# Batch 1's landmark sums from the loaded k and q, paired weight conversions and a new instruction order in a Nystrom attention and two-MLP kernel

## The chip, the cores and the metric

The kernel runs on one core of a Trainium2 chip, as one launch. The metric is the device time of a run in microseconds (us). A separate profiled execution gives the trace; its span runs from the first to the last instruction on the core.

## The reference, cut to what matters

```python
def _attn_ref(q, k, v):                      # (4, 8, 576, 64) each, float32
    m, scale = 32, 1.0 / np.sqrt(D)
    q_lm = q.reshape(B, H, m, S // m, D).mean(axis=3)      # landmarks: means of 18 tokens
    k_lm = k.reshape(B, H, m, S // m, D).mean(axis=3)
    A, Bm, C = sm(q, k_lm), sm(q_lm, k_lm), sm(q_lm, k)    # softmaxes of scaled products
    Z = Bm.transpose(0, 1, 3, 2) / (norm1(Bm) * norminf(Bm) + 1e-06)
    for _ in range(6):
        Z = 2 * Z - Z @ Bm @ Z
    return A @ Z @ C @ v

x = attention output as (2304, 512)
x = ((x @ w_a) * (x @ w_b)) @ w_out          # w_a, w_b: 512x1536, w_out: 1536x512
h = x @ w_in                                 # 512x2048
out = (h * np.tanh(softplus(h))) @ w_out2    # 2048x512
```

The weights come as float64, so each is loaded as pairs of 32-bit words and turned to float32 in the kernel.

## The kernel before, in words

**Two phases.** In the first, the attention of four batches is interleaved with the first MLP. `attention(ap, b, ...)` is a set of steps for batch b: `kl` and `ql` (landmark sums of k and q), `sB`, `BB` and `NS` (the small softmax and six steps of the inverse), `sC0`, `sC1` (landmarks against all keys), `ET0`, `ET1` (transposes by the unit matrix `ident`), `U`, `M`, and `A0`, `A1`, `A0n`, `A1n` (queries against landmarks, their exponentials and the normalised result `at`). `fold` (`f0`, `f1`, `F0`, `F1`) multiplies M into a tile of w_a and w_b and gives `bm`. A slot `s0` to `s11` (`ab`) makes the products of `at` and `bm` for both weights, and `o1` multiplies their product into w_out. The second phase is the second MLP and isn't touched.

**Weights.** `u0` holds units of the first MLP's weights. A unit's words are loaded into a staging tile (`stage`) and converted by `to_f32` in five instructions: Abs on ACT, two tensor_scalar and two scalar_tensor_tensor on DVE. A w_a/w_b unit is 128x512 elements; a w_out unit (`wo1_unit`) is split into two parts as well. `c0`, `c1`, ... in the order are such units, one instruction or two at a time. The first eight staging tiles are buffers of the tag `w`, which the w_out tiles take over later; further ones use three buffers of the tag `stg`.

**Order.** `ORDER_1` is a text that writes out the instruction order on ACT, PE and DVE by hand, up to slot 11: a name runs the next piece of batch 0's step, `+name` that of batch 1's step, `cN` that of a unit; a number is that many fill products of `ident` with itself; `|` closes one PSUM pool and opens the next. Each engine takes its queue in this order, so an instruction that waits holds up those behind it on its engine. After the text a loop over slots 12 to 95 with a list of due steps goes on. All loads are issued by SP; their place in SP's queue is the framework's choice.

**Batch 1's landmark sums before.** The host hands over q and k of batch 1 a second time, in token order (`q1`, `k1`). `load_tokens` loads them as six tiles `tok`. `lm_sum` multiplies each 126x128 block of tokens as weights by a 126x7 block matrix `blk`: 40 products into one PSUM bank for k and for q, each in two instructions in the trace. For batches 0, 2 and 3 a DVE reduction of the loaded tile (`kt`, `qt`) gives the sums. `kt` has a single buffer (tag `kv`), so batch 1's k is loaded when batch 0's last sC product has read the one before. It serves sC0 and sC1.

Of the kernel before, what the change touches and what calls it, by code (L numbers as in the profile page):

```python
# [17 lines left out]
LM = 32  # L18
# [13 lines left out]
def nystrom_moe_kernel(ctx: ExitStack, tc: tile.TileContext, q, k, v, w_a, w_b, w_out1, w_in2, w_out2, q1, k1, out):  # L32
# [55 lines left out]
    blk = const.tile([128, 7], F32, name="blk")  # L88
# [17 lines left out]
    def load_qk(ap, b):  # L106
        out, step = [], 4 if b else 2
        for src, nm, tag, bufs in ((k, "kt", "kv", 1), (q, "qt", "qt", 2)):
            t = ap.tile([128, 4, S], F32, tag=tag, bufs=bufs, name=nm)
            for j in range(0, 4, step):  # L110
                nc.sync.dma_start(out=t[:, j:j + step].rearrange("p j s -> p (j s)"), in_=src[b][:, S * j:S * (j + step)])
            out.append(t)
        return out

    def load_tokens():
        out = []
        for src in (k1, q1):
            ts = []
            for i in range(0, 5, 2):
                if src is q1 and i:  # L120
                    t = main.tile([128, 2, 2, S // 2], F32R, tag="AT", bufs=6, name="tok").bitcast(F32).rearrange("p a b s -> p (a b s)")
                else:
                    t = main.tile([128, 4, 288], F32, tag="x2", bufs=4, name="tok").rearrange("p a s -> p (a s)")
                w = min(2, 5 - i)
                nc.sync.dma_start(out=t[0:126, 0:DM * w], in_=src[:, DM * i:DM * (i + w)])
                ts.append(t)
            out.append(ts)
        return out
# [20 lines left out]
    def attention(ap, b, kt, qt, vt0=None, tokens=None):  # L149
# [226 lines left out]
    N_UNITS, N_SLOTS = 20, 12  # L376
    ORDER_1 = """
        kl kl ql ql c0 sB sC0 sB c0 sB sC1 4 c1 sC0 sB c2 sC1 BB 2 sC1 c3 BB sC1 sC1 c2 NS 2 c1 c3 NS ET0 NS
        c0 NS 2 c1 ET0 ET1 c3 c1 NS A0 ET1 NS c1 NS 1 A0 U NS A0 NS A0 c3 NS +kl U NS NS A0 c3 NS c0 +kl NS A0
        c0 NS +ql c2 c2 NS A0n c4 +ql NS +ql c5 c2 A0n M c6 +kl c5 M c5 A0n c5 f0 c7 A0n A1 c7 f0 c7 +kl A1 c8  # L380
        f0 +ql +kl A1 | s0 +ql c7 A1 +sC0 c5 +sC1 +sC0 s0 s0 A1 +sC1 s1 +sC1 A1 s0 c7 c6 s1 s1 A1n s0 s0 A1n
        c6 +sC1 s1 c6 +sC1 +sB c6 A1n +ET0 +sB s1 A1n +sB s1 +ET0 +sB s2 +ET1 c4 s2 c4 +BB c4 +ET1 s2 c4 +BB
        +U s2 c8 s2 +NS +U s2 s3 +NS +NS c8 +NS c8 s3 s3 +NS +NS c9 c8 +NS s3 f1 c8 c9 +NS +NS s3 c9 +NS c8 s3
        f1 c9 +NS c10 +NS f1 +NS +NS +NS s4 c10 c9 +NS s4 c10 s4 c9 +NS s5 s4 c10 s4 +M s5 s4 c10 s5 +M c9 c10
        s6 s5 c11 c10 +A0 s6 c11 s5 s6 c11 s5 c11 c12 s7 s6 c11 F0 s7 s6 +A0 c11 s6 s7 +A0 F0 +A1 c11 +A0 s7
        o0 F0 +A0 c12 o1 c12 +A0 c12 c12 o0 c13 F1 +A0n o1 s7 o2 c13 F1 s7 +A0n F1 +A0n o3 o2 +A0n c13 s8 c13
        c14 c13 o3 o4 s8 c14 c14 c14 c15 s8 +A1 o4 s9 c15 s8 o5 s9 +A1 s8 s8 c14 +A1 s9 c15 c15 c16 s10 s9 +A1
        c16 o6 c16 c16 s10 +A1 c15 s10 c16 o5 s11 +A1n o6 c17 o7 s9 s10 s11 +A1n s9 s10 c17 +A1n s11 s10 c17
        o7 c17 +A1n c18 s11 c18 s11 c18 s11 c17 c19 c18 c19 c19 c18 c19 c19
# [65 lines left out]
    def wab_units(g):  # L455
        def conv(i, jj, st):
# [3 lines left out]
            yield from to_f32(t[:, 2 * jj:2 * jj + 2, i], st, True)  # L460
            converted[g] = converted.get(g, 0) + 1
# [14 lines left out]
    def split_unit(dst_hi, dst_lo, st):  # L476
# [22 lines left out]
    def load_wo1(c):  # L499
        wo1[c] = main.tile([128, 2, DM], F32R, tag="w", bufs=8, name="wo1")  # L500
# [202 lines left out]
    u0 = Units(sum([wab_units(2 * w) + wab_units(2 * w + 1) + [wo1_unit(4 * w + c) for c in range(4)] for w in range(3)], []), early=8)  # L703
# [321 lines left out]
```

## Time and profile before

| | |
|---|---|
| median of 3 runs | 844.27 us (842.61 to 844.44) |
| the profiled execution's own time | 844.01 us |
| its span | 842.2 us |
| PE busy | 802.5 us (95%), 5882 matmuls |
| DVE busy | 555.0 us (66%) |
| ACT busy | 360.9 us (43%) |
| DMA | 183.45 MB, mean 218 GB/s |
| mean granted TensorE clock | 0.978 |

The profiled execution takes 1.81 us more than its span: that lies around the first and last instruction. A PE that is busy isn't a PE at its peak, because matmuls overlap and their ends are modelled. "Granted clock" is a share of 2.4 GHz; 0.50 is 1.2 GHz. A line L56 is the helper that records nearly every instruction of ACT, PE and DVE, so rows are told apart by their tiles. In the rows, a `MATMUL out<-moving,weights` is written with the names of its two operands; PEld is the weight load.

### The profile page before, as it was taken

What the parts mean: (1) busy time and instruction counts of PE and PEld (TensorE: products, weight loads), DVE (VectorE), ACT (ScalarE), POOL (GpSimd) and SP (SyncE); (2) the same over time, 40 slices, a digit from 0 to 9 for tenths busy, and PEclk for the clock granted to TensorE, in tenths of its full rate; (3) what the DMA queues carried; (4) which work ended last, traced back from release to release, by engine and by line L of the source; (5) the groups of instructions that cost most, each with busy time, mean ns of one, the idle gap of its engine ahead of it and who ended that gap; (6) DMA issues with size and microseconds to landing.
All of it is one profiled execution on the core that took longest, in us unless ns stands there. A gap on an engine that the chain in (4) does not pass through costs nothing.

```text
span 842.2 us, 14866 instructions
## 1 busy us (share of the span) xinstructions
PE 802.5 (95%) x5882; PEld 701.6 (83%) x5882; DVE 555.0 (66%) x1023; ACT 360.9 (43%) x826; POOL 146.9 (17%) x141
## 2 busy tenths in 40 slices
PE   5878899999999999999998899999999999999998
PEld 4765788987887887887887798998999999999997
DVE  7678887895574488788995678768443347433433
ACT  3555865434333444444543345345332234332332
POOL 0002022222231232222234435321000000000000
PEclk9679999999999999999999899999999999999999
DMA  9957577459326438777476866789755445655502
GB/s 326 334 203 255 179 241 234 176 195 317 107 86 243 179 96 295 266 264 251 131 255 252 293 249 245 271 318 340 262 194 219 165 174 211 219 213 194 187 1 75
DMA packets 48733, 183.45 MB, mean 218 GB/s; under 512 B 4260, under 2 KB 12452, under 8 KB 39320
## 3 DMA queue, kind: packets, MB, share of 16 engines
q1 hardware_dynamic: 48664, 182.51, 61.1%
q8 instruction: 46, 0.75, 0.4%
q14 instruction: 23, 0.19, 0.1%
HBM read 129.02 MB, written 53.48 MB: 217 GB/s over the span
## 4 chain that ended last, share of the span: by engine, by line
PE 73%; DVE 12%; DMA 7%; issue 3%; ACT 3%; POOL 0%; SPq 0%; DVEq 0%; ACTq 0%
PE ps_ab L56 32%; PE ps_o L56 20%; PE ps_bm L56 11%; PE ps_at L56 10%; DVE f L56 4%; DMA wi2d<-f 2%; DMA tok<-in_q_dram 2%; ACT sa L56 1%; DMA wo2d<-f 1%; DMA stg<-in_moe_w_a_dram 1%; DVE tg L56 1%; DVE f L413 1%; DVE wab L56 1%; ACT f L409 1%; DVE s L56 1%
## 5 line engine op out<-in xcount | busy, mean ns | idle before, releaser
L56 PE MATMUL ps_ab<-xc,wc 128*128 128x384 f32 x1008 | 199.8, 338 | 4.8 <-DVE u2s L56 3.1
L56 PE MATMUL ps_ab<-at,bm 128*128 128x288 f32 x1152 | 188.6, 304 | 6.0 <-DVE tg L56 4.8
L56 PEld LDWEIGHTS ps_ab<-xc,wc 128*128 128x128 f32 x1008 | 180.4, 189 | 16.1 <-DVE u2s L56 3.4
L56 PEld LDWEIGHTS ps_ab<-at,bm 128*128 128x128 f32 x1152 | 162.2, 190 | 31.3 <-issue 8.6
L56 PE MATMUL ps_o<-g,wo 128*128 128x288 f32 x1152 | 180.4, 298 | 5.7 <-DVE x2acc L56 2.6
L56 PEld LDWEIGHTS ps_o<-g,wo 128*128 128x128 f32 x1152 | 161.0, 189 | 20.4 <-issue 8.1
L555 POOL TENSOR_TENSOR g<-tg,g 128x288 fp32r<-128x288 f32 x96 | 85.7, 893 | 330.4 <-ACT g L56 330.4
L56 ACT ACTIVATE m<-c 128x384 f32<-128x384 f32 x96 | 50.3, 524 | 183.9 <-DVE c L56 183.9
L56 PE MATMUL ps_bm<-wo,g 128*128 128x512 f32 x288 | 94.4, 392 | 0.3 <-ACT g L56 0.3
L56 PE MATMUL ps_at<-wo,g 128*128 128x512 f32 x288 | 81.8, 391 | 0.0
L56 DVE TENSOR_TENSOR g<-m,g 128x384 fp32r<-128x384 f32 x96 | 66.2, 690 | 23.5 <-ACT g L56 23.5
L56 PE MATMUL ps_o<-wo,g 128*128 128x512 f32 x288 | 78.9, 391 | 0.0
L56 ACT ACTIVATE g<-tg 128x288 fp32r<-128x288 f32 x96 | 42.4, 442 | 75.5 <-DVE tg L56 75.1
L56 DVE SCALAR_TENSOR_TENSOR f<-stg,f 128x512 uint32<-128x512 uint32 x88 | 69.9, 797 | 1.5
L56 DVE TENSOR_TENSOR tg<-ps_ab,ta 128x288 f32<-128x288 f32 x96 | 43.3, 452 | 31.2 <-PE ps_ab L56 22.8
L56 PEld LDWEIGHTS ps_at<-wo,g 128*128 128x128 f32 x288 | 54.0, 188 | 10.0
L56 PEld LDWEIGHTS ps_o<-wo,g 128*128 128x128 f32 x288 | 53.5, 188 | 8.5
L56 ACT ACTIVATE ta<-ps_ab 128x288 f32<-128x288 f32 x96 | 38.8, 404 | 49.0 <-PE ps_ab L56 48.3
L56 PEld LDWEIGHTS ps_bm<-wo,g 128*128 128x128 f32 x288 | 53.4, 189 | 6.7 <-ACT g L56 0.8
L56 ACT ACTIVATE g<-m 128x384 fp32r<-128x384 f32 x96 | 50.2, 523 | 2.6
L56 DVE TENSOR_TENSOR c<-ps_ab,m 128x384 f32<-128x384 f32 x24 | 13.4, 557 | 48.2 <-PE ps_ab L56 48.2
L409 ACT ACTIVATE f<-stg 128x512 f32<-128x512 f32 x44 | 29.7, 675 | 31.7 <-DMA wi2d<-f 12.8
(145 smaller groups left out, 815.5 us busy)
## 6 DMA issues: line engine op xcount, KB each, us to landing
wc<-wcd SPq DMA_DIRECT2D x16, 1792.0 KB, 7.2
wo<-wod SPq DMA_DIRECT2D x16, 1024.0 KB, 5.4
stg<-in_moe_w_out_dram SPq DMA_DIRECT2D x28, 512.0 KB, 3.9
wcd<-wc SPq DMA_DIRECT2D x8, 1792.0 KB, 6.1
wab<-wabd SPq DMA_DIRECT2D x10, 1024.0 KB, 5.9
stg<-in_moe_w_in_dram SPq DMA_DIRECT2D x16, 512.0 KB, 5.8
wod<-wo SPq DMA_DIRECT2D x8, 1024.0 KB
stg<-in_moe_w_a_dram SPq DMA_DIRECT2D x12, 512.0 KB, 3.8
```

The costliest lines, as they stand in the source:

```text
L56: i = f(*a, **kw)
L409: i = ac.engine.activation(dst, hi.bitcast(F32), AF.Abs)
L413: i = ve.engine.tensor_scalar(dst, dst, F32_TINY, F32_HUGE, op0=ALU.max, op1=ALU.min)
L555: gp.tensor_tensor(t[:, 1], tg, t[:, 0].bitcast(F32), op=ALU.subtract)
```

## The change

Batch 1's `kl` and `ql` no longer use a second copy of k and q. Each is 18 products, one for every token t of a block, with `ident` as the weights and the 128x128 elements `[:, j, 18 l + t]` of the loaded `kt` or `qt` as the moving operand (four rows of 32, an element every 72 bytes); they accumulate in one PSUM bank, six products to a piece of the order. `load_tokens`, `blk`, `q1` and `k1` go. Four of the units, those of w_a and w_b for groups 0 and 1, become pairs: w_a's and w_b's 128x512 words lie side by side in a staging tile of twice the size, and each of the five instructions treats 128x1024 elements. The buffers of tag `w` become four of twice the size, and w_out tiles are two halves of one buffer. `u0.n` counts units finished in order, so that units may finish out of order. `ORDER_1` is a new text, with batch 1's `kl` and `ql` later: their first piece stands just before batch 0's A1 ends, the others after s0 has begun. Before, all of them but the last pieces stood ahead of s0.

```diff
-    blk = const.tile([128, 7], F32, name="blk")
...
-        ve.tensor_reduce(out=blk, in_=ident[:, 0:126].rearrange("p (l k) -> p l k", k=BLK), axis=AX, op=ALU.add)
...
-    def load_tokens():
-        out = []
-        for src in (k1, q1):
...
         def lm_sum(src, nm):
             x[nm] = sm([128, 4, LM], nm)
-            if tokens:
-                p, ts = bank("o1"), tokens[nm == "ql"]
-                for j in range(4):
-                    for i in range(5):
-                        n, r = (4, 72) if i == 4 else (7, 126)
-                        f0 = DM * (i % 2) + 128 * j
-                        pe.matmul(p[:, LM * j + 7 * i:LM * j + 7 * i + n], ts[i // 2][0:r, f0:f0 + 128], blk[0:r, 0:n], start=True, stop=True)
-                    yield
+            if b == 1:
+                p = bank("o1")
+                for t in range(BLK):
+                    pe.matmul(
+                        p[:, 0:128].rearrange("p (j l) -> p j l", l=LM), ident, src.rearrange("p j (l k) -> p k j l", k=BLK)[:, t],
+                        start=(t == 0), stop=(t == BLK - 1),
+                    )
+                    if t % 6 == 5:
+                        yield
                 ac.activation(x[nm].rearrange("p j l -> p (j l)"), p[:, 0:128], AF.Copy)
                 return
...
-    N_UNITS, N_SLOTS = 20, 12
+    N_UNITS, N_SLOTS = 16, 12
     ORDER_1 = """
-        kl kl ql ql c0 sB sC0 sB c0 sB sC1 4 c1 sC0 sB c2 sC1 BB 2 sC1 c3 BB sC1 sC1 c2 NS 2 c1 c3 NS ET0 NS
-        c0 NS 2 c1 ET0 ET1 c3 c1 NS A0 ET1 NS c1 NS 1 A0 U NS A0 NS A0 c3 NS +kl U NS NS A0 c3 NS c0 +kl NS A0
-        c0 NS +ql c2 c2 NS A0n c4 +ql NS +ql c5 c2 A0n M c6 +kl c5 M c5 A0n c5 f0 c7 A0n A1 c7 f0 c7 +kl A1 c8
-        f0 +ql +kl A1 | s0 +ql c7 A1 +sC0 c5 +sC1 +sC0 s0 s0 A1 +sC1 s1 +sC1 A1 s0 c7 c6 s1 s1 A1n s0 s0 A1n
...
+        kl kl ql ql sB sC0 sB sB sC1 4 sC0 c0 sB sC1 BB 2 sC1 c1 BB sC1 c0 NS 2 sC1 c0 NS NS ET0 c1 ET1 c0 ET0
+        NS 2 ET1 A0 c1 NS U NS A0 A0 c2 NS 1 c1 NS A0 NS c0 NS NS A0 NS c1 NS NS A0 NS U NS NS c3 A0n M M A0n
+        f0 c2 A0n A1 c3 f0 A0n f0 +kl A1 A1 | s0 +kl c2 s0 A1 c3 s0 c2 A1 +ql s0 c2 A1 +ql c3 +kl c4 s0 A1n
+        +ql s0 +kl A1n s1 +ql c3 +sC0 A1n s1 +sC1 +sC0 s1 +sC1 +sC1 A1n +sC1 s1 s2 +sC1 c4 c4 +sB s1 c4 f1 s2
...
     def stage(src, shape, early):
 
-        tag, bufs = ("w", 8) if early else ("stg", 3)
-        t = (main if early else base).tile([128, 512, 2], U32, tag=tag, bufs=bufs, name="stg")
+        if early:
+            t = main.tile([128, 2 * DM, 2], U32, tag="w", bufs=4, name="stg2")
+            v = t.rearrange("p (j i f) w -> p j i (f w)", j=2, i=2)
+            for i, a in enumerate(src):
+                nc.sync.dma_start(out=v[:, :, i], in_=a)
+            return t
+        t = base.tile([128, 512, 2], U32, tag="stg", bufs=3, name="stg")
...
-            yield from to_f32(t[:, 2 * jj:2 * jj + 2, i], st, True)
-            converted[g] = converted.get(g, 0) + 1
+            half = t[:, 2 * jj:2 * jj + 2]
+            yield from to_f32(half.rearrange("p j i f -> p (j i f)") if double else half[:, :, i], st, True)
+            converted[g] = converted.get(g, 0) + 1 + double
...
+    def wo1_tile(c):
+        if c % 2 == 0:
+            wo1_two[0] = main.tile([128, 2, 2, DM], F32R, tag="w", bufs=4, name="wo1")
+        wo1[c] = wo1_two[0][:, c % 2]
...
-    u0.prefetch(4)
-    vt0 = load_v(ap, 0)
-    tokens = load_tokens()
-    u0.prefetch(8)
+    u0.prefetch(2)
+    vt0 = load_v(ap, 0)
+    u0.prefetch(4)
     run0 = attention(ap, 0, kt, qt, vt0)
-    run1 = attention(ap, 1, *load_qk(ap, 1), None, tokens)
-    u0.prefetch(11)
+    run1 = attention(ap, 1, *load_qk(ap, 1))
+    u0.prefetch(7)
...
     def unit(n):
         yield from u0.units[n][2](u0.st[n])
-        u0.n = n + 1
-        if n > 7:
+        finished.add(n)
+        while u0.n in finished:
+            u0.n += 1
+        if n > 3:
             u0.prefetch(3)
```

## Rows read from the trace of the kernel before

**Rows 1.** Windows: start and end us, length, busy us of each engine, clock, DMA share, GB/s.
```profile
18.00:30.00 12.00, 9.74 (x200) 7.79 (x198) 9.50 (x24) 7.65 (x44) 0.00 (x0) 0.88 1.04 243
30.00:46.00 16.00, 16.00 (x108) 13.29 (x108) 9.11 (x19) 5.42 (x10) 0.00 (x0) 0.50 1.01 403
...
45.66:119.00 73.34, 62.81 (x670) 49.50 (x671) 63.10 (x135) 49.27 (x184) 11.28 (x13) 0.94 0.58 200
...
119.00:842.00 723.00, 705.12 (x4783) 624.20 (x4781) 460.96 (x815) 292.67 (x579) 134.32 (x116) 0.99 0.60 212
```

**Rows 2.** Chain that ended last, in order of time: start us, us, what.
```profile
13.44 15.94 DMA tok<-in_q_dram
...
29.43 1.59 PE ps_o L56 x6
...
31.38 4.36 PE ps_o L56 x20
...
41.45 4.36 PE ps_o L56 x20
45.80 1.65 PE ps_ab L56 x6
```

**Rows 3.** Tile `tok`: duration of one in ns (min/median/max), first and last start.
```profile
L56 PEld LDWEIGHTS ps_o<-blk,tok x80: 186/333/337, 23.1 to 45.4; 126*128 126x128 f32 x64, 72*128 72x128 f32 x16
L56 PE MATMUL ps_o<-blk,tok x80: 252/360/382, 23.1 to 45.4; 126*128 126x7 f32 x64, 72*128 72x4 f32 x16
```

**Rows 4.** Timeline of SP, then the DMA issues of 0 to 60 us (KB, us to landing).
```profile
27.11 3.62 SPq L399 DMA_DIRECT2D stg<-in_moe_w_out_dram  x3
31.67 0.33 SPq L111 DMA_DIRECT2D kt<-in_k_dram  x1
...
kt<-in_k_dram SPq DMA_DIRECT2D x1, 1152.0 KB, 13.9
```

**Rows 5.** Timeline, batch 0's last steps ahead of slot 0: start us, us, instructions.
```profile
26.55 0.22 DVE L56 TENSOR_TENSOR rz<-ps_at,rz 128x64 f32<-128x64 f32 x1
...
28.01 0.20 ACT L56 ACTIVATION_READ_ACCUMULATOR sa<-sa,stA 128x1 f32 x1
...
30.95 0.44 PE L56 MATMUL ps_at<-rz 32*32 32x32 f32 x16
...
38.53 1.96 PE L56 MATMUL ps_bm<-wab,mt 64*32 64x512 f32 x16
...
40.59 1.02 ACT L56 ACTIVATE bm<-ps_bm 128x1024 fp32r<-128x1024 f32 x1 [2.74 <-PE ps_bm L56]
...
42.32 1.19 DVE L56 TENSOR_TENSOR bm<-ps_bm,bm 128x1024 fp32r<-128x1024 f32 x1
```

**Rows 6.** Timeline of weight loads: fill products of 128 columns, then one stretch of `tok`.
```profile
7.55 2.64 PEld L56 LDWEIGHTS ps_o<-kl,ident 128*128 128x128 f32 x12 [7.55 <-issue]
...
12.87 1.20 PEld L56 LDWEIGHTS ps_o<-ident 128*128 128x128 f32 x8 [0.92 <-PE ps_p L56]
...
31.31 4.34 PEld L56 LDWEIGHTS ps_o<-blk,tok 126*128 126x128 f32 x20
```

**Rows 7.** Timeline of DVE, two reductions of the unit matrix.
```profile
1.51 0.28 DVE L56 TENSOR_REDUCE blk<-ident 128x7 f32<-128x126 f32 x1 [1.51 <-POOL ident masks.py:199]
1.71 0.36 DVE L56 TENSOR_REDUCE ist<-ident 128x32 f32<-128x128 f32 x1
```

**Rows 8.** Timeline of PE, the first and last of five waits between 53 and 66 us.
```profile
56.24 0.30 PE L56 MATMUL ps_at<-kl,ql 64*32 64x32 f32 x16 [3.38 <-ACT E L56]
...
65.86 0.43 PE L56 MATMUL ps_at<-rz 32*32 32x64 f32 x16 [0.90 <-DVE U L56]
```

**Rows 9.** Windows, two microseconds just after the longest of those waits.
```profile
58.00:60.00 2.00, 1.70 (x8) 1.60 (x8) 1.86 (x8) 0.65 (x4) 1.00 (x1) 0.50 0.00 0
```

**Rows 10.** Groups of DVE by form: busy us, mean ns of one, idle before.
```profile
L56 DVE SCALAR_TENSOR_TENSOR wab<-stg,wab 128x512 uint32<-128x512 uint32 x11 | 7.4, 687 | 0.1
...
L56 DVE TENSOR_TENSOR bm<-ps_bm,bm 128x1024 fp32r<-128x1024 f32 x5 | 6.1, 1212 | 0.0
```

More of the change, by code (lines that the diff above doesn't have):

```diff
@@ L31, in nystrom_moe_kernel @@
 @with_exitstack
-def nystrom_moe_kernel(ctx: ExitStack, tc: tile.TileContext, q, k, v, w_a, w_b, w_out1, w_in2, w_out2, q1, k1, out):
+def nystrom_moe_kernel(ctx: ExitStack, tc: tile.TileContext, q, k, v, w_a, w_b, w_out1, w_in2, w_out2, out):
     nc = tc.nc
@@ L112, in load_qk @@
             out.append(t)
-        return out
-    def load_tokens():
-        out = []
-        for src in (k1, q1):
[L118 to L127, printed above, removed]
         return out
@@ L147, in nystrom_moe_kernel, with attention @@
     PAIRS1 = {"ET0": "bm", "ET1": "bm"}
-    def attention(ap, b, kt, qt, vt0=None, tokens=None):
+    def attention(ap, b, kt, qt, vt0=None):
         x = {}
@@ L371, in attention @@
         return run
-    N_UNITS, N_SLOTS = 20, 12
+    N_UNITS, N_SLOTS = 16, 12
     ORDER_1 = """
-        kl kl ql ql c0 sB sC0 sB c0 sB sC1 4 c1 sC0 sB c2 sC1 BB 2 sC1 c3 BB sC1 sC1 c2 NS 2 c1 c3 NS ET0 NS
-        c0 NS 2 c1 ET0 ET1 c3 c1 NS A0 ET1 NS c1 NS 1 A0 U NS A0 NS A0 c3 NS +kl U NS NS A0 c3 NS c0 +kl NS A0
-        c0 NS +ql c2 c2 NS A0n c4 +ql NS +ql c5 c2 A0n M c6 +kl c5 M c5 A0n c5 f0 c7 A0n A1 c7 f0 c7 +kl A1 c8
-        f0 +ql +kl A1 | s0 +ql c7 A1 +sC0 c5 +sC1 +sC0 s0 s0 A1 +sC1 s1 +sC1 A1 s0 c7 c6 s1 s1 A1n s0 s0 A1n
[L382 to L389, printed above, removed]
@@ new lines, in nystrom_moe_kernel @@
+        +NS c5 s4 +ET1 s3 c5 +NS +U s4 +NS c5 +NS c4 s4 c5 s4 c6 +NS +U s5 +NS +NS c6 +NS s5 c6 s5 +NS +NS c7
+        c6 +NS s5 s6 +NS +NS s5 c7 +NS c7 s5 s6 s6 +NS c8 s7 c7 s6 +M s7 c7 s7 +M s6 c6 +A0 c7 s6 s7 c6 F1 c7
+        s7 +A0 s7 F1 +A0 +A1 F1 +A0 c6 F0 +A0 c8 c8 o0 +A1 +A0 c8 F0 +A0n o1 o0 c9 F0 o2 o1 +A0n +A1 +A0n o3
+        o2 +A0n +A1 c9 s8 c9 o3 c8 o4 s8 c9 c10 c9 +A1 s8 c10 c10 o4 s9 s8 +A1 c10 o5 c10 s9 s8 +A1n s9 s8 o5
+        c11 +A1n s10 s9 o6 +A1n c11 s10 c11 s9 c11 c12 s9 s10 c11 o6 s11 c12 s10 o7 c12 s11 c12 s10 c13 s10
@@ L390, in nystrom_moe_kernel @@
+        c12 s11 o7 c13 c13 s11 c13 s11 +A1n s11 c14 c13 c14 c14 c14 c15 c14 c15 c15 c15 c15
     """
     def stage(src, shape, early):
-        tag, bufs = ("w", 8) if early else ("stg", 3)
-        t = (main if early else base).tile([128, 512, 2], U32, tag=tag, bufs=bufs, name="stg")
+        if early:
[4 more added lines that the diff above has]
+            return t
@@ L453, in nystrom_moe_kernel, with wab_units @@
     wabd = [dram.tile([128, 2048], F32, name=f"wabd{g}") for g in range(6)]
-    def wab_units(g):
+    def wab_units(g, double=False):
         def conv(i, jj, st):
@@ L466, in wab_units @@
         for jj in range(2):
-            for i, w in enumerate((w_a, w_b)):
-                src = w.bitcast(U32)[256 * jj:256 * jj + 256, 512 * g:512 * g + 512].rearrange("(j p) f -> p j f", p=128)
-                out.append((src, 2, lambda st, i=i, jj=jj: conv(i, jj, st)))
+            two = [w.bitcast(U32)[256 * jj:256 * jj + 256, 512 * g:512 * g + 512].rearrange("(j p) f -> p j f", p=128) for w in (w_a, w_b)]
+            if double:
+                out.append((two, 2, lambda st, jj=jj: conv(0, jj, st)))
+            else:
+                for i, src in enumerate(two):
+                    out.append((src, 2, lambda st, i=i, jj=jj: conv(i, jj, st)))
         return out
@@ L485, in split_unit @@
         yield
-        (gp if u0.n == 36 else ve).tensor_tensor(dst_lo, f3, dst_hi.bitcast(F32), op=ALU.subtract)
-    wo1 = {}
+        (gp if u0.n == 32 else ve).tensor_tensor(dst_lo, f3, dst_hi.bitcast(F32), op=ALU.subtract)
+    wo1, wo1_two = {}, [None]
+    def wo1_tile(c):
+        if c % 2 == 0:
+            wo1_two[0] = main.tile([128, 2, 2, DM], F32R, tag="w", bufs=4, name="wo1")
+        wo1[c] = wo1_two[0][:, c % 2]
     wo1d = [dram.tile([128, 2, DM], F32, name=f"wo1d{c}") for c in range(12)]
@@ L492, in conv @@
         def conv(st):
-            wo1[c] = main.tile([128, 2, DM], F32R, tag="w", bufs=8, name="wo1")
+            wo1_tile(c)
             yield from split_unit(wo1[c][:, 0], wo1[c][:, 1], st)
@@ L499, in load_wo1 @@
     def load_wo1(c):
-        wo1[c] = main.tile([128, 2, DM], F32R, tag="w", bufs=8, name="wo1")
+        wo1_tile(c)
         nc.sync.dma_start(out=wo1[c].bitcast(F32), in_=wo1d[c])
@@ L702, in nystrom_moe_kernel @@
     consts()
-    u0 = Units(sum([wab_units(2 * w) + wab_units(2 * w + 1) + [wo1_unit(4 * w + c) for c in range(4)] for w in range(3)], []), early=8)
+    u0 = Units(sum([wab_units(2 * w, w == 0) + wab_units(2 * w + 1, w == 0) + [wo1_unit(4 * w + c) for c in range(4)] for w in range(3)], []), early=4)
+    u0.prefetch(2)
+    vt0 = load_v(ap, 0)
     u0.prefetch(4)
-    vt0 = load_v(ap, 0)
-    tokens = load_tokens()
-    u0.prefetch(8)
     run0 = attention(ap, 0, kt, qt, vt0)
-    run1 = attention(ap, 1, *load_qk(ap, 1), None, tokens)
-    u0.prefetch(11)
+    run1 = attention(ap, 1, *load_qk(ap, 1))
+    u0.prefetch(7)
     def fill(n):
@@ L716, in fill @@
             pe.matmul(p[:, 0:128], ident, ident, start=True, stop=True)
+    finished = set()
     def unit(n):
         yield from u0.units[n][2](u0.st[n])
-        u0.n = n + 1
-        if n > 7:
+        finished.add(n)
+        while u0.n in finished:
+            u0.n += 1
+        if n > 3:
             u0.prefetch(3)
@@ L1012 @@
         args.append(nc.dram_tensor(f"in_{name}_dram", a.shape, _mybir.dt.from_np(a.dtype), kind="ExternalInput").ap())
-    for name in "qk":
-        a = _np.pad(inputs[name].reshape(B, H, S, D)[1].transpose(1, 0, 2).reshape(S, DM), ((0, 54), (0, 0)))
-        a = arrays[f"in_{name}1_dram"] = _np.ascontiguousarray(a.reshape(5, 126, DM).transpose(1, 0, 2)).reshape(126, 5 * DM)
-        args.append(nc.dram_tensor(f"in_{name}1_dram", a.shape, _mybir.dt.from_np(a.dtype), kind="ExternalInput").ap())
     for i, (shape, dtype) in enumerate(_OUTS):
```

1 line of the change is left out of this document (added).

## The prediction

> **What bounds the kernel now.** I read the windows first. From 119 us, where the written order ends, to the last instruction TensorE is busy 705.12 of 723 us at a granted clock of 0.99 [rows 1]. Nothing in that part is touched, so a microsecond won or lost before it moves the end by about a microsecond. Ahead of it the picture is worse: between 18 and 30 us the DMA engines are full but move only 243 GB/s, and between 30 and 46 us TensorE is busy all the time, at 0.50 of its clock [rows 1].
>
> The chain says what that busy time is. From 13.44 to 29.38 us the last chain runs through the load of `tok`, then through `tok` products on TensorE, 20 of their instructions at a time, until the first product of slot 0 at 45.80 us in the chain's count [rows 2]. So batch 1's landmark sums hold the start of batch 0's slots. The tile view shows the price: 80 instructions between 23.1 and 45.4 us, with a median weight load of 333 ns [rows 3]. A stretch of 20 lasts 4.34 us, 0.217 us each [rows 6], so the 80 take up to 17.4 us.
>
> **What goes.** Three things leave the way to slot 0. First, 2,520 KB of `tok` loads: 126 rows x 5 blocks x 2,048 bytes, twice, or 2.58 MB. At the 243 GB/s of the time in which they move [rows 1] that is 10.6 us of transfers. Second, up to 17.4 us of TensorE. Third, the wait that these put on batch 0. Its fifth inverse step is finished by DVE at 26.77 us, but the sixth, in the same queue behind `tok` products that wait for data, starts at 30.95 us [rows 5]: 4.2 us lost. The fold's products start at 38.53 us, and its result is ready on DVE at 43.51 us [rows 5].
>
> Without `tok`, the sixth step can run at 26.8 us. Behind it the order needs its closing DVE work, M and MT (about 2 us), while ACT's last exponential of A0, which ends at 28.21 us [rows 5], releases A0n. I put the fold's start at 29.2 us. It needs 1.96 us on TensorE at the low clock, 1.02 on ACT and 1.19 on DVE [rows 5], 4.2 in all: `bm` is ready at about 33.5 us. That is the early bound for slot 0.
>
> The late bound comes from k. The first piece of `+kl` stands ahead of A1's end and of s0 on TensorE, and it now needs batch 1's `kt`. This load was issued at 31.67 us behind three w_out loads, and landed 13.9 us later [rows 4], at 45.6 us. With the `tok` transfers gone from the full DMA stretch it lands 10.6 us earlier, at 35.0 us; if it also goes ahead of the three w_out loads (1,536 KB, 3.9 us at the 403 GB/s of rows 1's second window) at 31.1 us. Behind it stand six products, 12 instructions, at 0.22 us (below): 2.6 us. So slot 0 starts between 33.7 and 37.6 us. I take the middle, 35.6 us, and against 45.66 us that is **10.0 us earlier** (8.1 to 12.0).
>
> **What comes.** 36 products with the unit matrix, each two instructions like the fill products, 72 in all. The trace has such products of 128 columns with a contiguous operand: eight weight loads in 1.20 us, 0.15 us each, and at the start twelve in 2.64 us, 0.22 us each [rows 6]. The strided operand isn't in the trace. Below, a read could be as cheap as the contiguous one, and I see no reason for less than 0.15 us. Above, the nearest rows are two DVE reductions of nearly as many elements: 0.28 us in contiguous order, 0.36 us with a step of 32 elements [rows 7], which is 29% more (it also writes 32 outputs where the other writes 7). By twice the price an instruction takes 0.30 us. I take 0.185 us, the middle of 0.15 and 0.22, because part of these products run at the low clock and a step may cost something.
>
> Six of the 36 stand ahead of s0 and are in its start above. The other 30, 60 instructions, stand among s0 and s1 and cost 60 x 0.185 = 11.1 us (9.0 to 18.0). From 45.66 to 119 us TensorE is idle 10.5 us of 73.34 [rows 1]. These products depend on nothing but k and q, so they fill waits they stand near. The five waits between 53 and 66 us, the first of 3.38 us and the last of 0.90 [rows 8], add up to 5.7 us, and I count these as filled. That leaves **5.3 us of lengthening**. Bounds: none, if all 10.5 us take them in at 9.0; 12.3, if a product costs 0.30 us. Filling the gap of 3.38 us should also spare the fall of the clock after it: at 58 to 60 us TensorE was busy 1.70 us at 0.50 [rows 9], of which half is lost, 0.85 us. I count **0.8 us back** (0 to 1.5).
>
> **Pairs.** A DVE instruction on 128x512 takes 687 ns, one on 128x1024 takes 1,212 [rows 10], so merging two saves about 0.16 us: four DVE instructions in four pairs, 2.6 us. I cost it at nothing. Over half of it lies ahead of slot 0, where DVE is busy 9.11 of 16 us [rows 1], and TensorE, not DVE, sets the pace there. Behind slot 0 it is about 1 us, and the new order leaves DVE about as much more conversion to do there (before, three more DVE steps of c5 and two of c7 stood ahead of `|`; now two first steps of pairs do). DVE is busy 63.10 of 73.34 us in that stretch [rows 1], so this cover is thin: if DVE were the bound, a microsecond would count either way. A pair also holds DVE's queue for up to 1.2 us, with batch 0's small inverse steps behind it; before, two units in succession held it as long.
>
> **At nothing, too.** The `blk` reduction (0.28 us) ran at 1.51 us [rows 7], before any k had come. The w_out tiles in halves of one buffer: the two halves are used by one `o1` piece and fall free together; if one load waited for the other's release, slots of the loop behind cover it. Units finished out of order change only when the next staging tile is loaded; DMA is full only 0.58 of that stretch [rows 1]. `kt` is held longer, and v of batch 1 loads into its buffer later, by the few us that sC1 comes later relative to s0.
>
> **Sum.** 10.0 - 5.3 + 0.8 = 5.5 us. From the profiled execution's own time of 844.0 us, of which 842.2 are span, that gives **838.5 us**. The median of the runs shown is 0.26 us above that execution, so the same number stands for both.
>
> **Rivals.** *The strided read takes twice as long.* Every element of the operand lies 72 bytes from the next, and rows 7 show that an engine can pay for steps. At 0.30 us the 60 instructions are 18.0 us, 12.3 beyond the five waits: 10.0 - 12.3 + 0.8 leaves a loss of 1.5 us, 845.5 us. Against it: at 0.22 us and the low clock there may be time for the read. The Trainium skill's page "SBUF — State Buffer", section "Door 1: The DMA port swizzle", speaks for this rival: at least two accesses must fall in each 16-byte line for full bandwidth, and here each falls in a line of its own. It gives no price for a miss; by it the time would be nearer this rival's than mine, and rows 7, a DVE and not a TensorE reading, agree only in direction.
>
> *The k load comes late (slower than before).* TensorE waits in order at the first `+kl`, with A1 and all slots behind it. My sum stays positive while slot 0 is less than 5.5 us later than 35.6, so while `kt` lands before 38.5 us; from 40.2 us on it is slower by over 0.2%. If SP issues it at 31.67 us as before and it again takes 13.9 us, it lands at 45.6 and slot 0 starts at 48.2 us: 12.6 us later than I say, 851 us. For it: that is where SP issued it, behind six `tok` and three w_out loads. Against it: what stood ahead of it was mostly a full DMA queue, which loses 2.58 MB.
>
> *Everything fits.* k is issued ahead of w_out, the products cost 0.15 us, and idle time takes them all in: 12.0 + 1.5, or 830.5 us. Against it: TensorE would have to be without idle time where 10.5 us of waits have several causes.
>
> *It doesn't matter.* Slot 0 starts early, but DVE, busy 86% of the stretch behind it, sets the end of the order, and the gain is lost in waits: 844 us. Against it: DVE has no more to do behind slot 0 than before, and starts on it earlier.
>
> **How the numbers follow.** The measurement can tell about 0.2%, 1.7 us, from no change. My forecast's own range, 832 to 842.5 us, gets 0.63 and everything-fits 0.11: faster 0.74. The doubled read 0.09 and the stretch set by DVE 0.06: within 0.2%, 0.15. The late k load, with landings from 40 us up, 0.11: slower. The range from 831 to 845.5 us leaves out the slower end and half of the everything-fits case, under 2 in 10.
>
> **What would show it.** Right: no DMA row of `tok`; DMA near 400 GB/s from 18 us on; `kt` of batch 1 landing by 35 us; the sixth inverse step near 27 us and slot 0's first product at 34 to 38 us; the `ident` products with k and q at 0.15 to 0.22 us an instruction; the order's last conversion near 113 us, and from there the same 723 us. Wrong: weight loads of `ident` 0.30 us apart; TensorE idle until `kt` lands past 38 us; more DVE idle time behind slot 0; the stretch behind the order longer than before, which would put the change of tiles, not the order, in question.

## The result, and the profile after

The changed kernel takes **850.87 us** (median of 8 runs, 849.05 to 854.05) where the kernel before, beside it, takes 844.36. The ratio is 1.0073, with a 95% interval of 1.0055 to 1.0091: 6.5 us slower, where 838.5 us was forecast. The profiled execution takes 849.37 us with a span of 847.6, 5.4 us more than the span before.

The chain of the kernel after, in order of time (start us, us, what):

```profile
4.42 10.19 DMA stg<-in_moe_w_b_dram
...
31.16 1.96 PE ps_bm L56 x16
33.12 0.96 PE ps_at L56 x16
34.09 3.22 PE ps_o L56 x12
...
41.78 11.53 PE ps_o L56 x48
```

`tok` is gone from it [rows 2]. In its place stands one block of 11.53 us: 48 instructions of the new landmark sums, without a gap. The timeline of TensorE tells what is around them:

```profile
28.42 0.44 PE L56 MATMUL ps_at<-rz 32*32 32x32 f32 x16 [1.51 <-DVE us L56]
...
31.16 1.96 PE L56 MATMUL ps_bm<-wab,mt 64*32 64x512 f32 x16 [0.66 <-ACT mt L56]
...
34.09 3.22 PE L56 MATMUL ps_o<-kt,ident 128*128 128x128 f32 x12
36.94 1.17 PE L56 MATMUL ps_ab<-at,bm 128*128 128x288 f32 x6
37.95 3.04 PE L56 MATMUL ps_o<-kt,ident 128*128 128x128 f32 x12
40.62 1.17 PE L56 MATMUL ps_ab<-at,bm 128*128 128x288 f32 x6
41.62 5.92 PE L56 MATMUL ps_o<-qt,ident 128*128 128x128 f32 x24
47.36 3.06 PE L56 MATMUL ps_o<-kt,ident 128*128 128x128 f32 x12
50.25 3.06 PE L56 MATMUL ps_o<-qt,ident 128*128 128x128 f32 x12
52.94 1.17 PE L56 MATMUL ps_ab<-at,bm 128*128 128x288 f32 x6
54.04 0.72 PE L56 MATMUL ps_at<-kt,ql 64*32 64x288 f32 x16
```

The sixth inverse step starts at 28.42 us and the fold at 31.16, 2.5 and 7.4 us before their times in [rows 5]. Slot 0 starts at 36.94 us, 8.7 us sooner than the 45.66 us that begins the third window of [rows 1]. But batch 1's first sC product, which needs the sums, starts at 54.04 us; in the trace before it stands at 47.38. So one chain is 8.7 us earlier and the other 6.7 us later.

Batch 1's k is issued by SP at 20.75 us and lands 13.3 us later, where [rows 4] had 31.67 and 13.9 (timeline of SP, then the row of the DMA issues):

```profile
20.75 0.33 SPq L109 DMA_DIRECT2D kt<-in_k_dram  x1
...
kt<-in_k_dram SPq DMA_DIRECT2D x1, 1152.0 KB, 13.3
```

The windows, with the columns of [rows 1], show the same from above:

```profile
18.00:30.00 12.00, 7.96 (x194) 5.70 (x193) 9.24 (x21) 8.78 (x46) 0.00 (x0) 0.78 1.04 408
30.00:46.00 16.00, 15.32 (x91) 11.47 (x89) 13.12 (x23) 9.64 (x43) 0.86 (x1) 0.86 0.49 185
45.66:119.00 73.34, 66.52 (x703) 53.81 (x702) 58.14 (x128) 44.20 (x150) 13.22 (x13) 1.00 0.54 188
119.00:842.00 723.00, 706.19 (x4764) 622.50 (x4764) 458.32 (x812) 291.15 (x574) 134.36 (x116) 1.00 0.59 210
```

The DMA engines now move 408 GB/s between 18 and 30 us where they moved 243, and TensorE's granted clock between 30 and 46 us is 0.86 instead of 0.50. The last row is the surprise. In the 723 us that were to stay as they were TensorE is as busy as before and its clock as high, yet it gets through 4,764 products where [rows 1] has 4,783.

The place of that loss is found with one tile. `u2s` is written once in each of the second MLP's 24 units. Its row in the tile view (duration of one in ns, first and last start in us), of the kernel before and then of the kernel after:

```profile
L56 DVE TENSOR_TENSOR u2s<-ps_ab,m x24: 545/557/558, 465.6 to 822.0; 128x384 f32<-128x384 f32 x24
```

```profile
L56 DVE TENSOR_TENSOR u2s<-ps_ab,m x24: 545/558/560, 466.5 to 826.9; 128x384 f32<-128x384 f32 x24
```

Before, 356.4 us lie between the first and the last; after, 360.4. A stretch that the diff doesn't touch is 4.0 us, 1.1%, slower. The windows from 600 to 800 us inside it, before and then after:

```profile
600.00:800.00 200.00, 200.00 (x1005) 180.84 (x1004) 84.76 (x155) 64.91 (x123) 0.00 (x0) 1.00 0.56 204
```

```profile
600.00:800.00 200.00, 200.00 (x992) 179.59 (x991) 83.62 (x152) 64.79 (x123) 0.00 (x0) 1.00 0.55 201
```

TensorE is busy all the time in both, at full clock, with 1,005 and 992 products. Worked out from the starts in the trace, in these 200 us, the mean distance from one `xc,wc` product to the next grows from 173.5 to 175.6 ns and from one `wo,g` product to the next, in `ps_o`, from 228.6 to 231.3 ns (in all three PSUM tiles that these fill, by 2.2 ns on the mean). With 1,008 and 864 such products in the phase that is about 4 us. The order of TensorE's, DVE's and ACT's queues is the same there in both kernels.

What differs there is where tiles lie. `blk`, 28 bytes a partition in a place of 32, was a constant. Without it the tiles that are laid out behind the constants move down by 32 bytes: `g2` from 26528 to 26496, `wo2` from 46496 to 46464, one of three `wc` buffers from 77216 to 77184. `xc` and the other two `wc` buffers stay. So the slower `xc,wc` products don't themselves read from another place: in the units whose `wc` buffer stayed, two of three, the distance grows from 173.3 to 175.7 and from 173.7 to 175.6 ns, and in the third from 173.6 to 175.5. By the starts and ends in the trace it grows as much, from 173.1 to 175.2 ns, where neither DVE nor ACT is at work at the same time.

The stages side by side, in us from the span's start (starts of a `tg` in the slots of the first MLP and of a `u2s` in the second):

| | before | after | difference |
|---|---|---|---|
| slot 0's first product | 45.66 | 36.94 | -8.7 |
| batch 1's first sC product | 47.38 | 54.04 | +6.7 |
| slot 15 (behind the written order) | 127.80 | 125.92 | -1.9 |
| slot 55 | 294.73 | 291.93 | -2.8 |
| second MLP, unit 0 | 465.62 | 466.55 | +0.9 |
| second MLP, unit 23 | 821.99 | 826.89 | +4.9 |
| last instruction | 842.2 | 847.6 | +5.4 |

Three losses are to be explained: what slots 0 to 15 give back, 3.7 us between slot 55 and the second MLP, and 4.0 us in the second MLP.

### The profile page after: what moved, and what is told of

Read it like the earlier page. It is cut to its first block, busy times and chain, and to the rows that moved or that the text cites. A ratio compares the mean times of both kernels' runs of the same rounds, so it can differ in the third digit from the quotient of the medians.

```text
span 847.6 us, 14815 instructions
## 1 busy us (share of the span) xinstructions
PE 805.2 (95%) x5874; PEld 700.7 (83%) x5874; DVE 550.5 (65%) x1006; ACT 360.9 (43%) x822; POOL 149.4 (18%) x141
## 4 chain that ended last, share of the span: by engine, by line
PE 80%; DVE 9%; DMA 5%; ACT 3%; issue 3%; SPq 0%; POOL 0%; DVEq 0%; ACTq 0%
PE ps_ab L56 34%; PE ps_o L56 24%; PE ps_bm L56 12%; PE ps_at L56 10%; DVE f L56 3%; DMA wi2d<-f 2%; ACT sa L56 1%; DMA stg<-in_moe_w_b_dram 1%; DMA wo2d<-f 1%; DVE tg L56 1%; DVE f L401 1%; DMA stg<-in_moe_w_out_dram 1%; DMA kt<-in_k_dram 1%; DVE xc L56 1%; ACT f L397 0%
## 5 line engine op out<-in xcount | busy, mean ns | idle before, releaser
L56 PE MATMUL ps_ab<-xc,wc 128*128 128x384 f32 x1008 | 203.0, 340 | 4.8 <-DVE u2s L56 3.1
L56 PE MATMUL ps_ab<-at,bm 128*128 128x288 f32 x1152 | 185.7, 301 | 6.0 <-DVE tg L56 3.7
L56 PEld LDWEIGHTS ps_ab<-at,bm 128*128 128x128 f32 x1152 | 160.3, 188 | 29.3 <-issue 7.9
L553 POOL TENSOR_TENSOR g<-tg,g 128x288 fp32r<-128x288 f32 x96 | 87.9, 916 | 330.0 <-ACT g L56 327.0
L56 DVE TENSOR_TENSOR g<-m,g 128x384 fp32r<-128x384 f32 x96 | 60.4, 629 | 25.6 <-ACT g L56 25.6
```

Of the source, the lines that this page charges most:

```text
L56: i = f(*a, **kw)
L553: gp.tensor_tensor(t[:, 1], tg, t[:, 0].bitcast(F32), op=ALU.subtract)
```

## The experiments

Three theories at first: *place* (the 32 bytes slow the second MLP), *strided read* (the new sums cost twice what contiguous products cost), and *queue order* (the new written order leaves a worse order of the queues behind it). Ratios are to the kernel before, run beside each on the same chip.

**1. after_pad32: the 28 bytes put back in the changed kernel, unused.**

```diff
+    blk = const.tile([128, 7], F32, name="blk")
```

> The changed kernel with the 28-byte tile blk allocated again in its old place and never used: on every engine the order of instructions is that of the changed kernel, but all tiles behind it in the left-hand pools lie 32 bytes higher again, as in the kernel before. Theory (place in memory): the 1.1% by which every matmul of the second MLP became slower (173 to 175.5 ns and 227 to 231 ns apart) comes from that shift, so they return to 173 and 227 ns and the time is about 847 us, 4 less than the changed kernel. Rival (the chip, the queues' order or the doubled buffers): the distances stay at 175 and 231 ns and the time stays at 850.9 us.

Measured: 847.26 us, ratio 1.0016 (1.0000 to 1.0032). The distances are 173.6 and 228.6 ns, and from the first `u2s` to the last 356.2 us:

```profile
L56 DVE TENSOR_TENSOR u2s<-ps_ab,m x24: 546/557/558, 468.6 to 824.8; 128x384 f32<-128x384 f32 x24
```

An unused tile gives the second MLP its pace back. In this execution the second MLP starts 3 us later than before; that is the second loss, still there.

**2. before_less32: the kernel before, with its `blk` in a buffer of another tag, so that the same tiles move down by 32 bytes (its staging tiles also change places with the buffers of that tag).**

```diff
-    blk = const.tile([128, 7], F32, name="blk")
+    blk = base.tile([128, 512], F32, tag="f24", bufs=2, name="f24")[:, 0:7]
```

> The kernel before with blk kept in a weight conversion buffer that is free at that time, so that the left-hand pools lie 32 bytes lower, as in the changed kernel; the order on every engine is that of the kernel before. Theory (place in memory): the second MLP's matmuls go from 173 and 227 ns apart to 175 and 231, and the time to about 848 us. Rival: 844.3 us.

Measured: 848.42 us, ratio 1.0037 (1.0022 to 1.0052), distances of 175.6 and 231.3 ns, 359.7 us from first to last `u2s`. With nothing else of the change, the kernel before gets the same slow second MLP. Place is shown both ways.

**3. before_plus32 and before_plus64: the kernel before with 32 and with 64 unused bytes more.**

```diff
+    pad = const.tile([128, 8], F32, name="pad")
```

> The kernel before with one more unused 32-byte tile, so that the left-hand pools lie 32 bytes higher than ever; the order on every engine stays. Theory (what matters is which half of a 64-byte unit a tile starts in): as slow in the second MLP as the changed kernel, about 848 us. Rival (the old place was no better than most, the changed one is a bad one): 844.3 us.

> The kernel before with an unused tile of 64 bytes: the left-hand pools lie 64 bytes higher, the order stays. Theory (64-byte units): matmuls of the second MLP 173 and 227 ns apart as in the kernel before, since the place within 64 bytes is the same. Rival (no such period; it depends on how tiles read at the same time lie to each other): another pair of distances.

Measured: at +32 bytes 847.41 us, ratio 1.0024 (1.0011 to 1.0038), with 175.8 ns for `xc,wc` and 227.4 for `wo,g`, and 358.7 us between the `u2s`. At +64 bytes, a single run: 850.17 us, 175.7 and 231.1 ns, 360.9 us. So it isn't a period of 64 bytes, and the two groups of products don't move together; of the four places tried the one of the kernel before is the best.

**4. second_phase_back and weights_back: 32 unused bytes in the second MLP's pool alone, in the changed kernel.** In the first they stand ahead of all its tiles, so that only staging and conversion tiles stay shifted (the constants lie in the same places in all these kernels); in the second behind `u3s`, so that `wo2`, the third `wc` buffer and `u4s` are back in place and `m`, `g2`, `u2s`, `u3s` are not.

```diff
     p2 = ctx.enter_context(tc.tile_pool(name="p2", bufs=1, side="left", reuse_waits="tile"))
+    p2.tile([128, 8], F32, name="pad")
```

> The changed kernel with 32 unused bytes at the start of the second MLP's own pool, so that all tiles of that pool (g2, m, u2s to u4s, wo2, the third wc buffer) lie where they lay in the kernel before, while the constants' and staging tiles stay 32 bytes lower, as in the changed kernel. Theory 1 (the place of the second phase's own tiles decides): the second MLP's products are back at 173.5 and 228.6 ns from start to start, and the time falls by some 3.6 us to 847. Theory 2 (the staging tiles s_in, s_out and the constants decide): they stay at 175.6 and 231.3 ns, and the time at 850 to 851 us.

> The same 32 bytes, but behind u3s in that pool: wo2, the third wc buffer and u4s lie where they lay before, while m, g2, u2s and u3s stay 32 bytes lower, with the staging tiles. If the second MLP's weight operands and moving weights decide: 173.5 and 228.6 ns. If the place of g2, m, u2s and u3s decides: 175.6 and 231.3 ns, as in the changed kernel. Values between, or one of the two groups back and the other not: it is the tiles' places relative to each other, and no one group.

Measured: second_phase_back 847.85 us, ratio 1.0049 (1.0026 to 1.0073); weights_back 850.57, ratio 1.0081 (1.0059 to 1.0103). The rows of `u2s`, first of second_phase_back, then of weights_back:

```profile
L56 DVE TENSOR_TENSOR u2s<-ps_ab,m x24: 545/558/559, 469.5 to 825.3; 128x384 f32<-128x384 f32 x24
```

```profile
L56 DVE TENSOR_TENSOR u2s<-ps_ab,m x24: 544/558/559, 466.4 to 827.0; 128x384 f32<-128x384 f32 x24
```

355.8 and 360.6 us: for the second MLP's pace its own tiles decide, not the staging tiles. The median of second_phase_back is only 2.0 us below the changed kernel's by the ratios, not clear of their intervals, and above after_pad32's. Whether the staging tiles' place costs something in the first phase, or this is chance, isn't settled: in its profile slot 15 comes at 128.31 us, at a granted clock of 0.95 from slot 0 to there, where the kernel after had 125.92 and 1.00. With only the weights back, `wo,g` has 232.9 ns, worse than in the changed kernel, and `xc,wc` 174.3, between the two. So no single group of tiles explains it; that it is how they lie to each other fits, but isn't shown.

**5. after_contiguous: each unit-matrix product reads 32 neighbouring elements.** Batch 1's landmarks are then sums of other elements than the reference's; the amount of work is the same.

```diff
-  src.rearrange("p j (l k) -> p k j l", k=BLK)[:, t],
+  src[:, :, LM * t:LM * t + LM],
```

> The changed kernel with the unit-matrix products reading 32 neighbouring elements of each row instead of every 18th, so batch 1's landmarks are sums of other elements; order and places in memory stay. Theory (the step costs reading time and TensorE sets the pace there): an instruction takes 0.15 us instead of 0.245, batch 1's sC0 starts 5 to 6 us earlier than 54.0 us, and the time is 4 to 6 us less than the changed kernel's 850.9. Rival (the step costs time that something else hides, DVE or the chain of batch 1): instructions 0.15 us apart, but under 2 us less in all. Second rival (not the step but the accumulation or weights make them slow): they stay 0.245 us apart.

Measured: 843.53 us, ratio 0.9993 (0.9973 to 1.0014), so 0.8% below the changed kernel's 1.0073. In its timeline of TensorE:

```profile
33.77 2.93 PE L56 MATMUL ps_o<-kt,ident 128*128 128x128 f32 x12 [0.95 <-DMA kt<-in_k_dram]
...
40.55 2.84 PE L56 MATMUL ps_o<-qt,ident 128*128 128x128 f32 x24
43.22 1.50 PE L56 MATMUL ps_o<-kt,ident 128*128 128x128 f32 x12
...
46.79 0.71 PE L56 MATMUL ps_at<-kt,ql 64*32 64x288 f32 x16
```

The same 24 instructions take 2.84 us instead of 5.92: 0.118 us each against 0.247. The windows of these two stretches, first of after_contiguous, then of the kernel after, show that the clock is not the reason, 1.00 in both:

```profile
40.50:43.40 2.90, 2.90 (x28) 2.90 (x27) 2.58 (x3) 2.90 (x21) 0.00 (x0) 1.00 0.00 0
```

```profile
41.60:47.50 5.90, 5.90 (x27) 5.19 (x26) 5.51 (x9) 3.38 (x18) 1.33 (x1) 1.00 0.00 0
```

At the low clock the two ways of reading differ little. The first 12 instructions of after_contiguous, at 33.77 us, run at a granted clock of 0.50 and take 2.93 us, where the 12 at 43.22 take 1.50 at the full clock. The window of the first:

```profile
33.77:36.35 2.58, 2.58 (x12) 2.58 (x13) 2.51 (x6) 0.00 (x0) 0.00 (x0) 0.50 0.95 314
```

The strided ones take nearly the same at either level, as the profile of weights_back shows, which has the same early part (two rows of its timeline, then the window of the first):

```profile
33.74 3.22 PE L56 MATMUL ps_o<-kt,ident 128*128 128x128 f32 x12 [0.93 <-DMA kt<-in_k_dram]
...
47.63 3.06 PE L56 MATMUL ps_o<-kt,ident 128*128 128x128 f32 x12
```

```profile
33.74:36.59 2.85, 2.85 (x13) 2.85 (x13) 2.78 (x7) 0.00 (x0) 0.00 (x0) 0.50 1.00 347
```

From start to start, within a stretch, a strided instruction takes 240 ns at 0.50 and at 1.00 alike, a contiguous one 213 and 112 ns. So the step's price shows only at the full clock.

Batch 1's sC product is 7.3 us sooner than in the changed kernel, and slot 15 stands at 120.91 us, 6.9 us before its place in the kernel before. The second MLP keeps its slow pace: 175.6 and 231.3 ns.

**6. pad32_late_order and before_other_late: the queue order behind the written order, exchanged.** Behind the written order the two kernels' queues differ in two stretches, in the trace before from 119 to 141 us and from 387 to 557 us, which reaches into the second MLP. Only the second stretch is exchanged. The first kernel is after_pad32 with the order that PE, DVE, ACT and POOL have there in the kernel before; the second is the kernel before with the changed kernel's order. It is forced by order-only dependencies (`LATE` is the list of instructions, engine by engine):

```diff
+    for engine, text in LATE.items():
+        seq = [traced[engine][int(n)] for n in text.split()]
+        for a, c in zip(seq, seq[1:]):
+            tc.add_manual_dep(c, a.name, mybir.DependencyInfo(mybir.DependencyClass.NoSync, mybir.DependencyReason.DATA), reason="late order")
```

> The changed kernel with the 32 bytes of blk restored, and from slot 56 to the middle of the second MLP's first third the order on TensorE, DVE, ACT and POOL forced to be that of the kernel before; the written order ahead is the changed one. Theory (queue order): the 2 to 4 us that the changed kernel and its padded form lose against the kernel before between slot 55 and the second MLP come from another order of conversions and slot instructions on DVE and ACT, which the framework chose there; with the old order the time is 843.5 to 845 us, 2 to 4 less than the padded kernel's 847.3. Rival (that stretch is bound by its conversions and gives back any earlier start): 847 us.

> The kernel before with the changed kernel's order forced on the four engines in that same late stretch; its written order, tiles and places stay. Theory (queue order): 847 to 848.5 us, 2 to 4 more than the kernel before. Rival: 844.9 us.

Measured: 845.97 us, ratio 1.0003 (0.9984 to 1.0022), and 846.69, ratio 1.0019 (0.9996 to 1.0042). Against after_pad32 the old order gives about 1.1 us, and in the kernel before the new one costs about 1.6 us. The direction is that of the queue-order theory, but both times lie between its range and the rival's, neither interval excludes no effect, and the forced profile still takes 174.9 us from slot 55 to the second MLP, where the kernel before took 170.9.

**7. sums_on_dve: batch 1's sums as four DVE reductions, as for the other batches, in pad32_late_order.**

> As pad32_late_order, but batch 1's landmark sums are four DVE reductions of the loaded k and q, as in the other batches, in place of the 36 unit-matrix products. Theory (TensorE's 17.6 us of strided products set the start of batch 1): DVE pays 5.4 us in a stretch where it is idle for about 9, batch 1's sC0 starts before 48 us instead of at 54.0, and the time is 5 to 8 us under that of pad32_late_order, 837 to 840 us. Rival (DVE becomes the bound, its queue waits for k at the first reduction and holds batch 0's steps): no less than pad32_late_order.

Measured: 844.26 us, ratio 0.9994 (0.9974 to 1.0014). Two of the reductions in its groups, and its window from 34 to 119 us:

```profile
L56 DVE TENSOR_REDUCE kl<-kt 128x64 f32<-128x1152 f32 x2 | 2.7, 1346 | 0.0
```

```profile
34.00:119.00 85.00, 71.22 (x700) 55.80 (x693) 73.44 (x146) 51.80 (x190) 13.64 (x14) 0.87 0.52 179
```

Slot 0 starts at 34.28 us, 11.4 earlier than before, but slot 15 at 124.76, only 3.0 earlier. DVE, with 5.4 us of reductions more, is busy 73.44 of 85 us, TensorE only 71.22, at 0.87 of its clock. That DVE now paces the order fits: DVE's results end 8.0 us of TensorE's waits in this window, against 4.0 in the kernel before from 45.66 to 119 us. No run tests it apart from the lower clock, and DVE's busy share, 86%, is that of the third window of [rows 1]. The expected 837 to 840 us were wrong. With the same forced order, the sums on TensorE read contiguously (permuted_late_order, experiment 9) stand at a ratio of 0.9905, so TensorE is the better engine for them.

**8. permuted_pad32: both losses mended, and the right sums.** The host hands over q, k and v of batch 1 with the tokens in the order (t, l) instead of (l, t), so that the products read neighbouring elements of the right tokens. Attention over all keys is the same in any order of the tokens, and batch 1's rows of the output go back to their places in transfers of 32 rows. The 28 bytes are put back. Beside it the changed kernel once more, as **after_again**.

```diff
-  src.rearrange("p j (l k) -> p k j l", k=BLK)[:, t],
+  src[:, :, LM * t:LM * t + LM],
...
+            a[1] = a[1].reshape(H, LM, BLK, D).transpose(0, 2, 1, 3).reshape(H, S, D)
```

> The changed kernel with the 28-byte tile put back, and with batch 1's tokens of q, k and v laid out so that each of the 36 x 2 unit-matrix instructions reads 32 neighbouring elements, and sums the right ones; batch 1's rows of the result are written back to their places by transfers of 32 rows. Theory (the strided read, 0.245 us against 0.118 us an instruction, and the shift by 32 bytes are the two losses): both are gone, batch 1's chain is ready some 7 us sooner than in the changed kernel, and the time is 839 to 841 us, a ratio of 0.993 to 0.996. Rival (VectorE paces the order's later part whatever the sums cost, and the early gain is lost again by the second MLP): 844 us or more, a ratio of 0.999 or above. A second rival: the shorter transfers of the result cost what the sums give back, which would show as a later end with the stages before it early.

> The changed kernel as it is, beside the one above on the same chip. Theory: 850 to 852 us, a ratio of 1.006 to 1.009, with the matrix products of the second MLP at 175.5 and 231 ns from start to start. Rival (the loss belongs to one chip): a ratio below 1.004.

Measured: permuted_pad32 **838.67 us, ratio 0.9928 (0.9907 to 0.9949)**, faster than both kernels; after_again 850.45 us, ratio 1.0073 (1.0049 to 1.0097), its distances 175.6 and 231.3 ns. The rows of permuted_pad32: TensorE's timeline, the tile view of `u2s`, and the window from 45.66 us.

```profile
38.32 2.84 PE L56 MATMUL ps_o<-qt,ident 128*128 128x128 f32 x24
...
44.56 0.72 PE L56 MATMUL ps_at<-kt,ql 64*32 64x288 f32 x16
```

```profile
L56 DVE TENSOR_TENSOR u2s<-ps_ab,m x24: 545/558/559, 460.3 to 816.4; 128x384 f32<-128x384 f32 x24
```

```profile
45.66:119.00 73.34, 66.29 (x693) 53.88 (x686) 62.08 (x133) 46.95 (x155) 13.80 (x14) 0.95 0.64 212
```

Slot 0 starts at 35.32 us, batch 1's sC at 44.56, 2.8 us sooner than before, slot 15 at 119.34, 8.5 sooner, and the second MLP takes 356.1 us. The two mends add up: the pad alone took 0.0057 off the ratio (4.8 us) and the contiguous reading alone 0.0080 (6.8 us), which from 1.0073 makes 0.9936, inside the interval.

**9. permuted_late_order, with permuted_again beside it: the old queue order in that version, forced in the same late stretch as in experiment 6 and not from slot 12 on, as the expectation has it.**

> The version with 32 neighbouring elements for each unit-matrix product and the 28-byte tile put back, with the queue order of the kernel before forced behind the written order (slot 12 to the second MLP). Theory (the order of the queues there costs the changed kernel about 2 us between slot 55 and the second MLP): 171 to 174 us from slot 55 to the second MLP, and a median some 2 us below the same version without it, 836 to 837.5 us. Rival (chance from one execution to the next): 174 to 176 us there, and a median within 1 us of the version without it.

> The same version without the forced order, as before, beside it on the same chip: 838 to 840 us, a ratio of 0.991 to 0.995, with 174 to 176 us from slot 55 to the second MLP by the one theory and anything from 171 to 176 by the other.

Measured: 836.68 us, ratio 0.9905 (0.9882 to 0.9927), and 837.47, ratio 0.9912 (0.9892 to 0.9932). Slot 55 to the second MLP takes 173.6 and 175.6 us in the two profiles, as the queue-order theory says; the medians are 0.8 us apart, as the rival says. Over all profiles of the study that stretch takes 170.9 to 174.9 us, mean 172.9, in the seven with the old order, and 172.6 to 175.8, mean 174.8, in the nine with the new one. Three timed pairs point the same way, by 1.1, 1.6 and 0.8 us, none outside its interval.

## Why the prediction was wrong, point by point

**"Nothing in that part is touched", and from there "the same 723 us": this step failed.** No instruction is touched, but the removal of `blk`, which the prediction costs only as a DVE reduction at nothing, moves the second MLP's tiles by 32 bytes, and its products come 1% further apart. That is 4.0 us by the rows of `u2s`, 4.8 us by the ratios with and without the pad. Experiments 1, 2 and 4 show it in both kernels. The prediction's last part named a longer stretch behind the order as a sign of being wrong, one that would put the change of tiles in question. That is what came, but through where unchanged tiles lie, not through anything that the changed tiles do. The step failed a second time between slot 55 and the second MLP, where the profile after takes 3.7 us more (below, under Open). Of the 10.9 us between the forecast gain of 5.5 and the profile's loss of 5.4 these two are 7.7; 3.6 arise ahead of slot 15, and the rest nearly cancels.

**The unit-matrix products, 0.185 us: the mis-sized term.** They take 0.247 by the stretch of 24. The 60 instructions behind s0, each stretch up to the start of what follows it, take 14.0 us instead of 11.1, 2.9 more. With this and with slot 0's 8.7 us the forecast sum of the early part, 5.5 us, becomes 1.3, where slot 15 is 1.9 us earlier. The rival of the doubled read, at a chance of 0.09, had the mechanism: at full clock, the strided read costs 2.1 times the contiguous one. It had the size too high, 0.30 us. The choice of 0.185 went wrong at the contiguous price and at the clock. The 0.15 [rows 6] is a mean of two paces, since the last six of those eight products are 0.11 us apart in the trace; at full clock a contiguous instruction takes 0.118, below the bound for which the prediction saw "no reason". And a strided one keeps a distance of 0.24 us at either level of the clock (experiment 5): at the low level the step costs little, but with these products at the high level, as here, it doubles the price. The rule that the prediction cites from the Trainium skill, "SBUF — State Buffer", section "Door 1: The DMA port swizzle" (fewer than two accesses to a 16-byte line cost bandwidth), agrees with the 2.1 in direction; it gives no figure to check.

**Slot 0 10.0 us earlier, at 35.6: right.** It is 8.7, at 36.94, inside the bounds of 33.7 to 37.6. k was issued at 20.75 us, still behind the three w_out loads, and landed at 34.1, where 35.0 was forecast for that order. The sixth step came 1.6 us later than forecast, because DVE finished the step before it later. The 12 instructions ahead of s0 took 3.22 us, not 2.6.

**5.3 us of lengthening and 0.8 back: right in kind.** (11.1 less 5.7 is 5.4; the slip has no weight.) Filling works: TensorE's idle time from 45.66 to 119 us falls from 10.5 to 6.8, at a clock of 1.00. How much of the 0.8 came back can't be told: in the other profiles of the changed order with the sums on TensorE the clock from slot 0 to slot 15 is 0.94 to 1.00, where the kernel before had 0.95. With contiguous reading the time from slot 0 to slot 15 changes by only -1.0 to 2.4 us in four profiles (1.9 in permuted_pad32); with the strided read it grows by 6.8, against a forecast of 4.5 net. What the sum left out is that batch 1's chain depends on the last of the 60: it started 6.7 us later, and the slots that need it followed.

**Pairs and w_out tiles at nothing:** not taken apart. The order with contiguous reading is 6.9 to 11.6 us ahead at slot 15 in four profiles, where the sum with the contiguous price of 0.118 gives 9.4, so no large cost shows there.

**The rivals.** The late k load gave 851 us, the measured time, by a mechanism that didn't occur: k landed early. "DVE sets the end" isn't what held this kernel back ahead of slot 15: cheaper sums on TensorE alone bring slot 15 forward by 5.0 us (after_contiguous). For sums_on_dve it fits. "Everything fits" comes near in its early part when the sums are read contiguously, but not in its time, because of what is lost behind slot 55. That permuted_pad32 ends at 838.67 us, almost the time that was forecast for the change itself, is luck: it stands 8.5 us ahead at slot 15, not 5.5, and loses 4.2 between slot 55 and the second MLP.

**Open.** Why 32 bytes matter: the distances grew with no other engine's help that the trace shows, and also for products whose own two operands had stayed in place. Which tiles must not lie how isn't settled. Between slot 55 and the second MLP the new order seems to cost 1 to 2 us, suggested by 16 profiles and three timed pairs, not shown by any one of them. The profiled execution of the kernel before was the fastest of all there, which makes the difference from it in that stretch, 3.7 us, larger than that of the two means, 1.9. The early difference of the queues, from 119 to 141 us, was never exchanged.

## What to carry to other kernels

Removing even a small, idle tile moves others: after any change of allocation, compare the start-to-start distance of unchanged products in the steady phase before you look for a cause in the part that you changed, and test with a pad. When an edit turns a copy in a handy layout into a strided read by TensorE, price the stride by a run, at the level of the clock that the products will have, and see whether the host can lay out the original so that the read is contiguous. And when products fill waits, ask which chain waits for the last of them.

## What the runs showed of the hardware that was not expected

- A shift of SBUF tiles by 32 bytes changes the distance of back-to-back float32 products at full clock: 173.5 to 175.6 ns (384 columns) and 228.6 to 231.3 ns (512 columns, those into `ps_o`). At +32 bytes the first grows and the second falls (175.8, 227.4), at +64 both grow (175.7, 231.1). In two of three units neither operand of the 384-column products had moved.
- At 1.00 of the clock, a float32 moving operand of 128 elements with 72 bytes from one to the next takes 0.247 us an instruction, one in runs of 32 neighbours 0.118.
- The strided instruction keeps its pace when the granted clock is halved, 240 ns from start to start at 0.50 and at 1.00; the contiguous one goes from 112 to 213 ns.
